# Batch 0 of a Fourier-mixing kernel: halved sums, its table transfers on another queue, some column sums moved into the main loop

## The chip, the cores and the metric

The kernel runs on one core of one Trainium2 chip. The metric is device time in microseconds (us) of one execution, the median of several. Before the change it is 1908.66 us (three runs, 1908.25 to 1909.99).

## The reference

Eight batches of 3008 x 256 numbers go through a two-dimensional Fourier transform of which the real part is kept; the result, 24064 rows of 256, goes through a gated feed-forward layer.

```python
def _attn_ref(x):                      # x: (8, 3008, 256) float32
    X = np.fft.fft(x, axis=1)
    X = np.fft.fft(X, axis=2)
    return X.real.astype(np.float32)

def _moe_ref(x, w_gate, w_val, w_out): # x: (24064, 256); weights (256, 1536), (256, 1536), (1536, 256)
    gate = 1.0 / (1.0 + np.exp(-(x @ w_gate)))
    val = x @ w_val
    return (gate * val @ w_out).astype(np.float32)
```

The weights arrive as 64-bit floating-point numbers; x and the result are float32.

## The kernel before, in words

**Stages.** Per batch the transform along the sequence is a matrix product with cosine and sine tables. The 3008 rows are folded by symmetry first, so that 753 rows (kept as 128 partitions x 6 "sets" q, row 6p + q) and 753 columns k are left; even and odd k stand apart in the tables ST[0] (cosine) and ST[1] (sine), 377 and 376 columns. The results are two arrays, pk and qk, of 128 features by 1505 frequencies. The transform along the features is never carried out: it is multiplied into w_gate and w_val ("merge"), which gives G1 and G2. The main loop then runs over 576 steps (8 batches x 6 chunks of 252 frequencies x 12 slices of the hidden width). In step i TensorE computes G1 by pk (front_a) and, a step's work later, G2 by qk on top (front_b), in a PSUM tile pf; ScalarE saves twice the first part in a tile ae (part); sums and differences of both give frequency k and its mirror image. Sigmoid (ScalarE) and products (VectorE) follow in gate_a and gate_b, and the output product comes five steps behind (back).

**E.** Feature 128 is alone in its symmetry class and has a row of its own, E, one partition high. It is written to DRAM (ed), and read back spread over 128 partitions as ek (e_rows, line 755); ScalarE starts pf with it (seed, line 765) from step 5 on. In steps 0 to 4 the first 252 of its columns (e0) are multiplied in by TensorE.

**Order.** Nothing is scheduled by a program: the order in which the source calls things is the order in each engine's queue, and each engine takes its queue strictly in order. Buffers come from pools with a fixed number of tiles per tag; a tile that is asked for again waits until all uses of the old one have ended. Matter for the change: pool hp, tag h (three buffers; the raw weight blocks 0, 1 and 2 take them first, later the gate results h), pool zp, tag z, and pool app, tag ae (two each), and the PSUM banks (three in rotation under tag x, five fixed ones po0 to po4). side, gap, mid and spare are lists of work to be issued in a given step; at(i, f) adds to the end of step i.

**The start, which the change rewrites.** Before step 0 the kernel has to

- load x of batch 0 (load_rows, line 191), the tables (load_table, line 194) and the weight blocks (weight_load, line 328), all on SP's queue in the order of the source; the table dt of the feature transform comes on ScalarE's queue;
- fold x (half_rows, line 573; VectorE) in the order of SLICES (line 485), two sets, two sets, one, one;
- turn each weight block from 64-bit to float32: weight_parts (ScalarE, lines 382 and 383), weight_join (three operations of VectorE, lines 392 to 395, then one of GpSimd, line 397);
- merge the first two blocks (merge, line 410): eight matmuls of 256 columns in the records, then two copies by ScalarE (lines 417, 418) to G2 and G1;
- sum over the sets (half, line 595): per table and per half of the columns, the even sets into one bank ev, the odd ones into another, od, 24 matmuls of 377 or 376 columns;
- add and subtract ev and od into pk and qk (places, line 611): the sum gives the near columns k, up to 752, and the difference the far ones, 1504 - k;
- the same for E (e_sums, line 696).

Every matmul is on line 133, in the helper mm, so the rows of the profile are told apart by the tiles: ev, od and pe are the sums, ps a merge, pf the front of a step, po the output. In float32 each matmul has two records.

The near columns of the first two chunks are all that the first 24 steps read.

## Time and profile before

| | |
|---|---|
| median of three runs | 1908.66 us |
| the profiled execution: its time | 1909.15 us |
| its span | 1907.4 us |
| clock granted to TensorE | 1.0 throughout |
| TensorE busy | 1895.6 us, 99% of the span |
| VectorE, ScalarE, GpSimd busy | 80%, 71%, 81% |
| first records of pf (front matmuls) | weights from 32.73, matmul from 33.05 us |
| transfers in the first 60 us | 15.58 MB |

The span runs from the first to the last recorded instruction; the 1.75 us to the execution's time lie around it. "Busy" of TensorE is modelled from the starts of pipelined matmuls. In the timeline, rows of equal instructions that follow each other are merged (x8 is eight records), and what stands in brackets is the idle time before a row and what ended it. PEld is the load of the stationary operand, which goes on beside the matmuls; SPq is SP's queue, which issues transfers. In the page's chain of waits each piece follows from what released it.

### The profile page before, as it was taken

The numbers are of one execution on the slowest core, as the hardware profiler recorded it, in microseconds if no ns is written. First come the engines' busy times: TensorE is split into PE (matmuls) and PEld (weight loads), VectorE is DVE, ScalarE is ACT, GpSimd is POOL, SyncE is SP. The second block draws the span as 40 slices with busy tenths as digits, with TensorE's granted clock in tenths as the row PEclk, the third lists the DMA queues.
The fourth block names the chain that finished last, engine by engine and source line by source line (L and its number), as shares of the span: only waits on it lengthen the run. The fifth ranks groups of instructions, "written<-read, shape, count | busy, mean of one in ns | idle before, by whom it ended". The sixth has DMA issues, their size and how long they took to land.

```text
span 1907.4 us, 36057 instructions
## 1 busy us (share of the span) xinstructions
PE 1895.6 (99%) x11836; PEld 1756.6 (92%) x11836; DVE 1520.6 (80%) x3375; ACT 1353.2 (71%) x3235; POOL 1543.4 (81%) x2733
## 2 busy tenths in 40 slices
PE   8999999999999999999999999999999999999999
PEld 5788999999999999999999999999999999999998
DVE  7678888878979778897788878888788777977775
ACT  4777777777777777777777777677767777777775
POOL 2489879987999779997799878999789986877770
PEclk9999999999999999999999999999999999999999
DMA  8446221212022121211211212122120110010001
GB/s 315 120 134 80 71 89 51 72 33 81 21 64 54 31 87 32 62 41 37 89 39 48 45 39 81 40 52 58 30 74 17 36 37 15 15 25 17 15 18 30
DMA packets 197333, 109.33 MB, mean 57 GB/s; under 512 B 134823, under 2 KB 188818, under 8 KB 195354
## 3 DMA queue, kind: packets, MB, share of 16 engines
q1 hardware_dynamic: 196568, 106.50, 21.1%
q8 instruction: 95, 1.56, 0.3%
q14 instruction: 92, 0.75, 0.1%
q10 hardware_dynamic: 546, 0.51, 0.1%
q0 software_dynamic: 32, 0.00, 0.0%
HBM read 71.24 MB, written 47.87 MB: 62 GB/s over the span
## 4 chain that ended last, share of the span: by engine, by line
PE 94%; DMA 2%; SPq 1%; POOL 1%; ACT 1%; DVE 0%; issue 0%; ACTq 0%; POOLq 0%
PE pf L133 49%; PE po L133 41%; PE sum L133 2%; DMA rtab<-in_stab_dram 1%; PE ps L133 1%; POOL sf L824 1%; DMA st<-in_stab_dram 1%; SPq L206 1%; DMA raw<-in_moe_w_val_dram 0%; PE od L133 0%; POOL x L507 0%; SPq L192 0%; SPq L375 0%; PE pe L133 0%; PE ev L133 0%
## 5 line engine op out<-in xcount | busy, mean ns | idle before, releaser
L824 POOL TENSOR_TENSOR sf<-h,sf 128x168 f32<-128x168 f32 (+1 forms) x1104 | 621.0, 582 | 79.5 <-DVE h L818 75.9
L824 POOL TENSOR_TENSOR sf<-h 128x168 f32<-128x168 f32 (+1 forms) x920 | 519.3, 584 | 159.8 <-DVE h L818 158.0
L133 PE MATMUL pf<-qk,G 128*128 128x252 f32 (+1 forms) x2304 | 583.4, 376 | 0.9 <-ACT ae L787 0.8
L133 PE MATMUL pf<-pk,G 128*128 128x252 f32 (+1 forms) x2304 | 582.7, 376 | 0.0
L772 ACT ACTIVATE pf<-ek,ge 128x252 f32<-128x252 f32 (+1 forms) x1142 | 538.2, 471 | 23.2 <-DMA ge<-G 3.0
L133 PE MATMUL po<-sf,wf 128*128 128x168 f32 (+1 forms) x2944 | 508.3, 305 | 0.0
L787 ACT ACTIVATE ae<-pf 128x504 f32<-128x504 f32 (+1 forms) x576 | 338.8, 588 | 218.7 <-PE pf L133 217.2
L133 PEld LDWEIGHTS pf<-pk,G 128*128 128x128 f32 x2304 | 435.9, 190 | 53.3 <-ACT pf L772 1.5
L133 PE MATMUL po<-h,wf 128*128 128x168 f32 (+2 forms) x2584 | 461.3, 307 | 0.0
L133 PEld LDWEIGHTS po<-sf,wf 128*128 128x128 f32 x2944 | 453.4, 190 | 8.0
L818 DVE TENSOR_TENSOR h<-pf,z 128x252 f32<-128x252 f32 (+1 forms) x576 | 240.4, 417 | 274.0 <-ACT pf L815 270.5
L802 DVE TENSOR_TENSOR z<-ae,pf 128x504 f32<-128x504 f32 (+1 forms) x576 | 384.6, 668 | 83.1 <-ACT h L801 79.1
L908 DVE TENSOR_TENSOR c<-c 128x168 f32<-128x168 f32 (+1 forms) x920 | 438.7, 500 | 3.3
L133 PEld LDWEIGHTS pf<-qk,G 128*128 128x128 f32 x2304 | 410.6, 190 | 32.3 <-ACT ae L787 2.1
L133 PEld LDWEIGHTS po<-h,wf 128*128 128x128 f32 x2584 | 410.4, 190 | 17.8 <-issue 0.9
L801 ACT ACTIVATE h<-pf 128x252 f32<-128x252 f32 (+1 forms) x576 | 216.9, 376 | 146.3 <-PE pf L133 129.0
L815 ACT ACTIVATE pf<-z 128x252 f32<-128x252 f32 (+1 forms) x576 | 214.3, 372 | 116.4 <-DVE h L814 114.5
L814 DVE TENSOR_TENSOR h<-h,pf 128x252 f32<-128x252 f32 (+1 forms) x576 | 232.9, 404 | 0.0
L824 POOL TENSOR_TENSOR sf<-sf 128x168 f32<-128x168 f32 (+1 forms) x184 | 101.7, 553 | 14.4
L824 POOL TENSOR_TENSOR sf<-sf,h 128x168 f32<-128x168 f32 (+1 forms) x184 | 110.1, 598 | 0.0
L891 ACT COPY c<-po 128x504 f32<-128x504 f32 (+1 forms) x138 | 78.5, 569 | 0.0
L918 DVE STREAM_TRANSPOSE os<-c 128x256 f32<-128x256 f32 x188 | 76.5, 427 | 0.1
(158 smaller groups left out, 876.4 us busy)
## 6 DMA issues: line engine op xcount, KB each, us to landing
x<-xr SPq DMA_DIRECT2D x14, 1536.0 KB
out_dram<-os SPq DMA_DIRECT2D x376, 56.0 KB
xr<-in_xf_dram SPq DMA_DIRECT2D x105, 128.0 KB
x<-x SPq DMA_DIRECT2D x112, 96.0 KB
xr<-in_xf_dram SPq DMA_DIRECT2D x14, 384.0 KB
ek<-ed SPq DMA_DIRECT2D x40, 126.0 KB
out_dram<-os SPq DMA_DIRECT2D x288, 7.0 KB
xr<-in_xf_dram SPq DMA_DIRECT2D x21, 124.0 KB
```

Of the source, the lines that this page charges most:

```text
L133: nc.tensor.matmul(o, l, r, start=start, stop=stop, skip_group_check=True)
L772: nc.scalar.activation(PF[i][:, g], EK[i // NFT], AF.Copy, scale=ge[:, g, f : f + 1])
L787: nc.scalar.activation(AP[i], PF[i], AF.Copy, scale=2.0)
L801: nc.scalar.activation(H[p][:, fh, 0:n], PF[i][:, 0], AF.Sigmoid)
L802: nc.vector.tensor_tensor(z[:, :, ::-1], AP.pop(i), PF[i], op=ALU.subtract)
L814: nc.vector.tensor_tensor(h[:, fh, 0:n], h[:, fh, 0:n], pf[:, 1], op=ALU.mult)
L815: nc.scalar.activation(pf[:, 0], z[:, 0], AF.Sigmoid)
L818: nc.vector.tensor_tensor(h[:, fh, n:], pf[:, 0], z[:, 1], op=ALU.mult)
L824: nc.gpsimd.tensor_tensor(block(p, dst), block(p, a), block(p, b), op=(ALU.subtract, ALU.add)[op])
L891: (nc.vector.tensor_copy if t == 1 or t == 3 else nc.scalar.copy)(C[0][:, 3 * t * R : 3 * (t + 1) * R], PO[t][:, 0 : 3 * R])
L908: nc.vector.tensor_tensor(t[:, dst * R : (dst + 1) * R], *v, op=(ALU.subtract, ALU.add)[op])
L918: nc.vector.transpose(os_[0][0][:, s, 0:nb, h, :], t[:, c0 : c0 + nb * TB])
```

## The change

All of it concerns batch 0.

- **Halved sums.** For an even row s the table's columns k and 752 - k differ by sign alone, and the sign goes with s mod 4. So only the columns from 188 up (of the even k) and up to 375 (of the odd k), H0 to H1 in the table, 377 in all, are loaded and summed for even sets, once for rows that are 0 and once for rows that are 2 modulo 4, in banks x and y; unfolded gives all columns as x + y and, mirrored, x - y. To have one kind of row in a set, sets 0 and 2 of x are loaded with the odd partitions exchanged (two transfers of 64 partitions each), and so are the table's (load_mixed). Set 4 has both kinds; its table comes as two tiles with zeros in every other partition (load_apart, in columns of wf that are free).
- **Order.** SLICES is now set 4, sets 0 and 2, set 5, set 1, set 3. The even sets of cosine and sine are summed first. E's sums stand in one place, behind the folds, on four strips of the array.
- **Queues.** x comes first on SP's queue; the even tables and one odd one are issued by ScalarE; dt and the weight blocks 0 and 1 come on SP behind x and between the last odd tables.
- **Merges** of blocks 0 and 1 stand behind the sums, one of them behind the other's join; twelve and three matmuls on a cleared tile stand before the sums (warm). The copy of e0 goes from ScalarE to VectorE.
- **Far columns** of pk, of the even k of qk, and of E, and E's way through DRAM are issued in steps 1 to 3 (E's row is read back in step 2).
- ST[0] has to be whole for the other batches' E at step 40, so its even sets are loaded again at step 35 (load_again).

```diff
-    def load_rows(q, n):
-        nc.sync.dma_start(out=X[0][0:NP, :, q : q + n], in_=xf[0, :, :, q : q + n])
-    def load_table(t, q, n, lo=0, hi=NE + NO):
-        nc.sync.dma_start(out=ST[t][0:NP, q : q + n, lo:hi], in_=stab[:, t, q : q + n, lo:hi])
+    def load_rows(*qs):
+        for q in qs:
+            for ps, r in ((slice(0, NP, 2), q), (slice(1, NP, 2), 2 - q)) if q in (0, 2) else ((slice(0, NP), q),):
+                nc.sync.dma_start(out=X[0][ps, :, q], in_=xf[0, ps, :, r])
+    H0, H1 = NE // 2, NE + NO // 2
+    def load_table(t, q, start=nc.sync.dma_start):
+        start(out=ST[t][0:NP, q], in_=stab[:, t, q])
+    def load_mixed(t):
+        for ps, qs in ((slice(0, NP, 2), slice(0, 3, 2)), (slice(1, NP, 2), slice(2, None, -2))):
+            nc.scalar.dma_start(out=ST[t][ps, 0:3:2, H0:H1], in_=stab[ps, t, qs, H0:H1])
+    apart = [[wf[:, 2 * t + h].rearrange("p m n -> p (m n)")[:, 6 * WC : 6 * WC + NE] for h in range(2)]
+             for t in range(2)]
+    def load_apart(t):
+        for h in range(2):
+            nc.scalar.dma_start(out=apart[t][h][h:NP:2], in_=stab[h::2, t, 4, H0:H1])
+    def load_again():
+        nc.sync.dma_start(out=ST[0][0:NP, 0:NQ:2], in_=stab[:, 0, 0:NQ:2])
...
-    turns = itertools.count()
+    turns = itertools.chain((2, 3), itertools.cycle((2, 3, 4)))
     def weight_use(j):
         w, c = jobs[j]
         if w == 2:
             WO[c] = WS.pop(j)
         else:
-            merge(WS.pop(j), w, c, (4, 2, 3)[next(turns) % 3] if j > 1 else None)
-    def merge(ws, g, c, other):
+            merge(WS.pop(j), w, c, HELD.pop(j) if j in HELD else bank("ps", next(turns)))
+    HELD = {}
+    def merge(ws, g, c, ps):
         cs = slice(c * WC, (c + 1) * WC)
-        ps = bank("ps", other)
...
-    SLICES = ((0, 1), (2, 3), (4,), (5,))
+    SLICES = (slice(4, 5), slice(0, 3, 2), slice(5, 6), slice(1, 2), slice(3, 4))
...
+    def unfolded(f, x, y, sn=False):
+        nc.vector.tensor_tensor(f[:, H0:H1], x[:, 0:NE], y, op=ALU.add)
+        two = [t[:, 1:NE].rearrange("p (b n) -> p b n", b=2) for t in ((y, x) if sn else (x, y))]
+        nc.vector.tensor_tensor(f[:, 0 : 2 * H1].rearrange("p (b n) -> p b n", b=2)[:, :, H0 - 1 :: -1], *two,
+                                op=ALU.subtract)
+    def seq_sums(what, x, y, od):
+        d = PQE[0][what]
+        w = [W[0, blk][what] for blk in range(2)]
+        cols = (H0, NE - H0, 0), (NE, NO // 2, NE - H0)
+        turn = {}
+        def add(n, key, o, w, tab, first=True):
+            turn[key] = turn.get(key, 0) + 1
+            mm(o, w, tab, turn[key] == 1 and first, turn[key] == n)
+        def even(*qs):
+            for q in qs:
+                for blk, (lo, n, to) in enumerate(cols):
+                    for h in range(2):
+                        if q == 4 or h == q // 2:
+                            tab = apart[what][h][0:NP, to : to + n] if q == 4 else ST[what][0:NP, q, lo : lo + n]
+                            add(2, (h, blk), (x, y)[h][:, to : to + n], w[blk][:, q], tab, blk == 0)
+        def odd(q, *blks):
+            for blk in blks or range(2):
+                lo, n = ((0, NE), (NE, NO))[blk]
+                add(3, blk + 2, od[blk][:, 0:n], w[blk][:, q], ST[what][0:NP, q, lo : lo + n])
+        def copy():
+            a = evp.tile([P, NE], F32, name="a", tag="a")
+            nc.scalar.copy(a, y[:, 0:NE])
+            return a
+        def join(a):
+            f = hp.tile([P, 6 * WC], F32, name="u", tag="h") if what else wf[:, 0].rearrange("p m n -> p (m n)")
+            unfolded(f, x, a, what)
+            return lambda blk, *ends: places(d, blk, what == 1, f[:, blk * NE : NE + blk * NO],
+                                             od[blk][:, 0 : NE - blk], ends)
+        return even, odd, copy, join
...
+    def e_first():
+        ps = bank("pe")
+        cols = (H0, NE - H0, 0), (NE, NO // 2, NE - H0)
+        turn = {}
+        def add(q, blk, band):
+            lo, n, to = cols[blk] if band < 2 else ((0, NE, 0), (NE, NO, 0))[blk]
+            tab = apart[0][band][0:NP, to : to + n] if q == 4 else ST[0][0:NP, q, lo : lo + n]
+            k = turn[band, blk] = turn.get((band, blk), 0) + 1
+            mm(ps[band * TB : band * TB + 1, to : to + n], W[0, blk][2][:, q], tab,
+               k == 1 and (blk == 0 or band > 1), k == (3 if band > 1 else 2))
+        def sums():
+            for odd, even in ((5, 0), (1, None), (3, 4)):
+                for blk in range(2):
+                    if even is not None:
+                        for h in range(2):
+                            add(even or 2 * h, blk, h)
+                    if blk == 0:
+                        for b in range(2):
+                            add(odd, b, 2 + b)
+        def unfold():
+            er = op.tile([P, NK + 1], F32, name="er", tag="os")[0:1]
+            nc.vector.memset(er[:, NK:], 0.0)
+            y, *o = (pool.tile([P, 2 * CH], F32, name=tag, tag=tag)[0:1, 0:NE]
+                     for pool, tag in ((zp, "z"), (zp, "z"), (app, "ae")))
+            for i, t in enumerate((y, *o)):
+                n = NE - i // 2
+                nc.scalar.copy(t[:, 0:n], ps[(i + 1) * TB : (i + 1) * TB + 1, 0:n])
+            f = ST[0][0:1, 4:6].rearrange("p q k -> p (q k)")
+            unfolded(f, ps[0:1], y)
+            def part(*ends):
+                for blk in range(2):
+                    places(er, blk, False, f[:, blk * NE : NE + blk * NO], o[blk][:, 0 : NE - blk], ends)
+            def end():
+                part(1)
+                nc.sync.dma_start(out=ed[0:1], in_=er)
+            part(0)
+            return er, end
+        return sums, unfold
...
-    nc.scalar.dma_start(out=dt, in_=dtab.rearrange("(c p) d -> p c d", p=P))
     load_x(0)
-    for j in range(2):
-        weight_load(j)
-    load_rows(0, 2)
-    load_table(0, 0, 2)
-    load_rows(2, 2)
-    load_table(1, 0, 2, 0, NE)
-    load_table(0, 2, 2)
-    load_rows(4, 1)
-    load_table(0, 4, 1)
-    load_rows(5, 1)
-    weight_load(2)
-    load_table(1, 2, 2, 0, NE)
-    load_table(0, 5, 1)
-    load_table(1, 4, 2, 0, NE)
-    load_table(1, 0, NQ, NE)
-    for j in (3, 5, 6, 8, 9, 4, 7):
+    idle = wf[:, 0].rearrange("p m n -> p (m n)")[:, 0 : P + WC]
+    for t in (idle, *apart[0], *apart[1]):
+        nc.vector.memset(t, 0.0)
+    load_rows(4, 0, 2, 5, 1, 3)
+    for t in range(2):
+        load_apart(t)
+    for t in range(2):
+        load_mixed(t)
+    load_table(0, 5, nc.scalar.dma_start)
+    load_table(0, 1)
+    load_table(1, 1)
+    nc.sync.dma_start(out=dt, in_=dtab.rearrange("(c p) d -> p c d", p=P))
+    weight_load(0)
+    load_table(0, 3)
+    weight_load(1)
+    load_table(1, 5)
+    load_table(1, 3)
+    for j in (2, 3, 5, 6, 8, 9, 4, 7):
         weight_load(j)
     e0 = shared["qk"][:, 4 * WC : 4 * WC + CH]
     nc.gpsimd.memset(e0, 0.0)
+    def warm(o, n):
+        for i in range(n):
+            mm(o[:, 0:WC], idle[:, 0:P], idle[:, P:], True, True)
+    warm(bank("warm", 2), 12)
+    seq_start(0)
+    folds = iter(fold_ops(0, 2))
+    od_c = [bank("od", t) for t in range(2)]
+    even, odd, copy, join = seq_sums(0, bank("u"), bank("u"), od_c)
+    e_, e_unfold = e_first()
+    od_s = [bank("od", 4)]
+    even_s, odd_s, copy_s, join_s = seq_sums(1, bank("u", 2), bank("u", 3), od_s)
+    for q, n in (((4,), 3), ((0, 2), 0)):
+        next(folds)()
+        even(*q)
+        even_s(*q)
+        warm(od_c[0], n)
+    a, a_s = copy(), copy_s()
+    next(folds)()
+    odd(5)
+    for f in folds:
+        f()
+    pk = join(a)
+    HELD[0] = bank("ps")
+    od_s.append(bank("od"))
+    odd(1)
+    odd_s(1, 1, 0)
+    odd(3)
+    for blk in range(2):
+        pk(blk, 0)
     weight_parts(0)
+    weight_join(0)
+    e_()
+    odd_s(5)
+    odd_s(3, 1)
     weight_parts(1)
-    weight_join(0)
+    weight_use(0)
+    qk = join_s(a_s)
     weight_join(1)
-    warm = bank("warm", 2)
-    for i in range(4):
-        mm(warm[:, 0:WC], dt[:, 0, 0:P], dt[:, 0], True, True)
-    weight_use(0)
+    er, e_end = e_unfold()
+    weight_parts(2)
+    nc.vector.tensor_copy(e0[0:1], er[:, 0:CH])
+    HELD[1] = bank("ps", 3)
     weight_use(1)
-    seq_start(0)
-    cos = [seq_group(0, blk, 0, (2 * blk, 2 * blk + 1)) for blk in range(2)]
-    e_, e_even = e_sums(1)
-    sin = [seq_group(0, 0, 1)]
-    for q, f in zip(SLICES, fold_ops(0, 2), strict=True):
-        f()
-        e_(*{1: (0, 1), 5: (2, 3, 4, 5)}.get(q[-1], ()))
-        sin[0][0](*{5: (3,)}.get(q[-1], ()))
-        cos[0][0](*q)
-        cos[1][0](*q)
-        sin[0][0](*{1: (0, 1), 4: (2,), 5: (4, 5)}.get(q[-1], ()))
-    places_c = [cos[blk][1]() for blk in range(2)]
-    weight_parts(2)
+    odd_s(3, 0)
     weight_join(2)
-    rest, *ends = e_even()
-    rest()
-    for f in ends:
-        f()
-    for f in places_c:
-        f()
-    nc.scalar.copy(e0[0:1], E0[0][:, 0:CH])
+    qk(0, 0)
+    qk(1, 0, 1)
     weight_parts(3)
     weight_join(3)
-    sin.append(seq_group(0, 1, 1, (0, 1)))
-    sin[1][0](*range(NQ))
     for j in range(KEEP, KEEP + 3):
         weight_load(j)
-    places_s = [group[1]() for group in sin]
-    for f in places_s:
-        f()
-    e_rows(0)
...
+    at(35, load_again)
...
+    at(1, lambda: qk(0, 1))
+    at(1, e_end)
+    at(2, lambda: e_rows(0))
+    for blk in range(2):
+        at(2 + blk, lambda blk=blk: pk(blk, 1))
```

places and the tail of e_sums (now e_joint, for the other batches alone) stay as they were; half and seq_group, which served batch 0 alone, are gone.

## The prediction

> **What bounds the kernel now.** I read the page's busy times, then its chain of waits, then the timeline and the chain of the first 60 us, because the edit touches nothing but the first four steps and one transfer at step 35.
>
> ```profile
> PE 1895.6 (99%) x11836; PEld 1756.6 (92%) x11836; DVE 1520.6 (80%) x3375; ACT 1353.2 (71%) x3235; POOL 1543.4 (81%) x2733
> ```
>
> TensorE is busy all the time, so the length is its work plus the part of the start in which it cannot work. The chain of waits over the first 60 us says where that part ends:
>
> ```profile
> 14.43 9.31 DMA st<-in_stab_dram
> ...
> 26.05 2.10 PE od L133 x6
> 28.15 0.63 PE ev L133 x2
> 28.79 0.63 PE od L133 x2
> 29.42 1.90 PE ev L133 x6
> 31.32 1.90 PE od L133 x6
> 33.21 4.25 PE pf L133 x20
> ```
>
> Up to 23.7 us transfers decide; from there TensorE runs without a pause, and the first front matmul (pf) comes at 33.0. Behind it the chain is TensorE alone (bar a stall of 0.6 us near 147 us), so a shift of the first pf reaches the end. The edit is therefore priced by when that first pf comes. Its prices stand in the timeline (start, duration):
>
> ```profile
> 5.03 0.66 ACT L382 ACTIVATE raw<-raw 128x512 f32<-128x512 f32 x1 [2.80 <-DMA raw<-in_moe_w_gate_dram]
> 5.79 3.48 PE L133 MATMUL warm<-dt 128*128 128x256 f32 x8 [5.79 <-DMA dt<-in_dtab_dram]
> ...
> 12.59 1.99 PE L133 MATMUL ps<-raw,dt 128*128 128x256 f32 x8 [1.58 <-POOL raw L397]
> ...
> 15.38 1.21 DVE L494 TENSOR_TENSOR x<-x 128x1020 f32<-128x1020 f32 x1
> ...
> 19.49 0.68 DVE L494 TENSOR_TENSOR x<-x 128x510 f32<-128x510 f32 x1
> ...
> 22.01 0.68 DVE L494 TENSOR_TENSOR x<-x 128x510 f32<-128x510 f32 x1
> ...
> 24.80 0.43 DVE L392 TENSOR_SCALAR raw<-raw 128x512 f32<-128x512 f32 x1 [0.19 <-ACT raw L382]
> 25.26 0.43 DVE L393 TENSOR_SCALAR raw<-raw 128x512 int32<-128x512 int32 x1
> 25.72 0.69 DVE L395 SCALAR_TENSOR_TENSOR raw<-raw 128x512 int32<-128x512 int32 x1
> ...
> 26.55 1.28 POOL L397 TENSOR_TENSOR raw<-raw 128x512 int32<-128x512 int32 x1 [14.02 <-DVE raw L395]
> ```
>
> From fold to fold VectorE takes 4.1 us for two sets (15.38 to 19.49) and 2.5 us for one (19.49 to 22.01). Preparing one weight block takes VectorE 0.46 + 0.46 + 0.69 us and GpSimd 1.3 us; its merge takes TensorE 1.9 us with its tail. A sum of 377 columns comes every 0.63 us. Transfers of the first 60 us, in slices of 1.5 us, keep to 361 to 416 GB/s from 4.5 to 36 us, whether their pieces are of 1, 2 or 3 KB:
>
> ```profile
> GB/s 0 105 340 408 393 416 394 382 382 398 395 376 361 367 375 381 375 384 389 388 384 395 376 392 302 204 305 351 282 14 1 3 0 6 150 119 38 60 0 0
> ```
>
> **What the change removes.** TensorE: 24 sums of 0.63 us (15.1) become 16 of half the columns and 12 whole ones. A 189-column matmul is in no row: at least half of 0.63, at most the 0.42 of the 252-column pf; I take 0.32, as the other sums go by columns. That is 5.0 + 7.6 = 12.6 us, 2.5 less. E's matmuls run four abreast on strips of the array (8 of them in 1.44 us); the 20 new ones have three of 377 columns on the longest strip, 1.9 us against 2.25 now. Transfers: 1.1 MB less ahead of the first step (12 table sets become 6 whole and 6 half ones), at 0.385 MB/us (the row below) 2.9 us less; the two weight blocks that stood first now stand behind x and most tables. Both gains count only if TensorE or the transfers still decide.
>
> **What it moves, and the new path.** Eight completion counters are dealt out in turn to the transfers of SP and ScalarE together, and an issue waits until its counter's last transfer has landed. Set 4 of x is first on SP; like the 512 KB weight block that is first now (issued 0.74, used 5.03), it lands at about 5.1. The second halves of x are issued only then: one counter is set 4's, the next an apart table's on ScalarE (issued from 2.1, behind the table load and VectorE's clears; landed 5.7). A 512 KB transfer needed 4.3 us of which 1.35 are its bytes, so 2.9 us are fixed: 256 KB issued at 5.2 land at 8.8, the next, sharing the engines with ScalarE's tables, at about 9.7. Then:
>
> - VectorE folds sets 0 and 2 together (4.1) and 5, 1, 3 one by one (7.6): 9.7 to 21.4. It is one unbroken queue, and everything below stands behind it.
> - join(a), 2 operations of 0.46 with a wait each: 22.5. The od bank of the sine is the first u bank, freed here; TensorE's sums of sets 1 and 3 mostly wait anyway.
> - two near-column sums of pk, 0.92: 23.4. The odd set 3 has to be summed by then; its table lands at 21.4 and its fold ends at 21.4, two arrivals on one point.
> - weight block 0, 1.61 + 0.15 to the hand-over: 25.2; GpSimd 1.3: 26.5. TensorE is free at the same point: set 3 (1.3) from 21.5, E (1.9), three sine sums (1.9) give 26.6.
> - merge 0, 1.9: 28.5. Now the new wait: join_s writes a tile of pool hp, whose three buffers hold the raw weight blocks 0, 1 and 2; it takes block 0's, which merge 0 reads. It begins only at 28.5, and VectorE's weight block 1 stands behind it in program order: 29.5, then 31.3; GpSimd 32.6.
> - merge 1, 1.72 to its successor: 34.4; the last sine sum 0.63: 35.1. TensorE has nothing else from 28.4 to 32.7, an idle stretch of 4.3 us that is not there now.
>
> First pf 35.2 against 33.0: **+2.2 us**. The saved 2.9 us of TensorE and the earlier tables (last one 24.8) lie in waits.
>
> **Steps 0 to 4.** E's temporaries now live until e_end at step 1: one of the two ae buffers is held, so part(1) on ScalarE has to wait until z has read AP[0] (0.68 us, VectorE, itself behind weight blocks 3, 5 and 6), and front_b(1) waits for it. Setting the listed durations in order gives a pause of about 0.8 us there: **+0.8**. Bounds: 0, if z is early, and 1.5. The five far-column operations (0.46 each, 2.3 us) and the copy of e0 that ScalarE hands to VectorE go to VectorE in steps 0 to 3, where it is idle about a third of the time (5.3 us of 10 busy from 50 to 60 us): 0 while that cover lasts, else their 2.3. E's row is written to DRAM at step 1 and read back at step 2, both on SP behind ge and the xr copies. Issued 48.5 and 53.3, it lands at 57.3, and seed(5) wants it at 57.6: hidden, with a margin near 1 us by the row's readers, and each us beyond costs one. Nothing on SP behind the read is due before.
>
> **Later.** load_again moves 1.1 MB (2.9 us) on SP at step 35; its reader, e_joint, is five steps of 3.1 us on. What stands behind it on the queue are output stores, which already wait up to 4 us without holding TensorE: 0, up to 0.5. ScalarE issues nine transfers of 0.49 us and then waits for a counter until about 8.6; its first copy is due at 15: 0. The 12 + 3 warm matmuls end before the first sums or fill a pause: 0.
>
> Sum: 2.2 + 0.8 = +3.0. The profiled execution took 1909.15 us (its span 1907.4 and 1.75 around it), 0.5 above the median 1908.66: 1912.2 in its own terms, **1911.7** as a median. From no change a measurement here tells about 0.2%, 3.8 us.
>
> **A rule against it: the clock.** The four warm matmuls took 3.48 us, the next eight-record groups 1.89: TensorE begins at half speed (though the granted clock reads 1.00 there) and is quick after about 3.3 us. A pause of 1.6 us (11.0 to 12.6) did not bring this back; no row shows one of 4.3. By these rows the sum stays +3.0. [...]
>
> **Rivals.**
>
> 1. *Transfers and TensorE still decide (faster).* If VectorE's chain lay beside them, both merges would be done when the last table lands (24.8), and four sums of 0.63 would remain: first pf at 27.4, -5.6, with +0.8 behind it 1903.9. For it: the present chain names only transfers and TensorE. Against: it decides only if weight block 1 leaves GpSimd before 24.8, 8 us sooner than the queue of folds, merge 0, join_s allows. Chance 0.04.
> 2. *The clock falls in the new pause.* Merge 1 and what follows run at half speed for 3.3 us, costing 1.7 (up to 3.4 over two stretches): 1913.4, up to 1915.1. Chance 0.25.
> 3. *64-row transfers are slow.* x sets 0 and 2 and the even tables (2.1 of 7.9 MB) go in every-other-row halves, which no row shows. At full rate nothing is added; at half rate 5.5 us, ahead of everything: 1917.2. For full rate: 32-row copies between SBUF rows with 512-byte pieces reach 190 GB/s beside other traffic, so neither end is excluded. I take full rate, since no size of piece has slowed the slices above. Chance 0.13. [...]
> 4. *Absorbed.* The start slips, but the ae pause vanishes and the stall at 147 us (0.6) takes up a part: +1.6, 1910.3. Chance 0.10.
>
> **How the numbers follow.** The forecast as worked out has 0.48; its own range is +2.0 to +4.5 (E's row late by one, the ae pause at its bounds), a third of it above 3.8. Slower by over 0.2%: 0.16 + 0.21 of rival 2 + 0.13 of rival 3 = 0.50. Faster: 0.04. Within: 0.46. The range leaves out rival 1 and the ends of 3: 1909.9 to 1916.8.
>
> **What would show it.** Right: first pf near 35; VectorE without a pause from about 10 to 25; TensorE idle some 4 us between two groups of ps, ended by GpSimd's raw; join_s right behind merge 0's end; ae of step 1 waiting for VectorE. Wrong: the ps groups close together, pf before 31 (rival 1); ps records at twice their length behind the pause (2); the first double fold beginning after 11 (3). A late e_joint or a wait for ek at step 4 would refute the zeros.

## The result, and the profile after

The kernel before took 1909.11 us (median of six runs, 1908.25 to 1910.0), the changed one 1918.18 (six runs, 1917.46 to 1919.96): 9.1 us slower, a ratio of 1.0048 with a 95% interval of 1.0035 to 1.0061. The forecast was 1911.7, its range 1909.9 to 1916.8: the sign was the likelier one, the size was three times too small and outside the range. The profiled execution took 1917.46, its span 1915.6 and 1.86 around it.

The busy times of the page say nothing of the cause; TensorE is as full as it was:

```profile
PE 1902.0 (99%) x11870; PEld 1765.9 (92%) x11870; DVE 1527.9 (80%) x3394; ACT 1351.6 (71%) x3232; POOL 1542.9 (81%) x2733
```

The chain of waits over the first 75 us (start, duration, what) shows the new path, with the pieces left out that add nothing:

```profile
1.70 4.29 DMA wf<-in_stab_dram
...
6.01 4.62 DMA x<-in_xf_dram
...
10.83 1.22 DVE x L513
...
20.11 4.30 PE od L133 x12
24.41 2.01 PE pe L133 x20
26.42 2.10 PE od L133 x6
28.51 1.74 PE ps L133 x8
30.35 0.56 DVE u L615
30.93 0.55 DVE u L617
...
32.34 0.69 DVE raw L413
...
34.50 3.78 PE ps L133 x8
38.28 1.26 PE od L133 x2
39.53 4.86 PE pf L133 x20
44.40 3.47 PE ps L133 x16
47.87 0.68 DVE z L871
48.58 0.60 ACT ae L856
49.22 1.12 PE pf L133 x4
```

To be seen: merge 0 (28.51), then join_s on VectorE (30.35), then weight block 1 (raw), then merge 1 at 34.50. Before, pf started at 33.0; now at 39.3 (the chain dates its piece from the predecessor's end). The waits of TensorE hold the pause, and the row of merge 1 its price. The waits list total, times and the longest in us; the timeline start, duration and, in brackets, the idle time before a row and what ended it:

```profile
PE ps L133 <- POOL raw L415: 4.3, 1, 4.3
```

```profile
28.35 1.89 PE L133 MATMUL ps<-raw,dt 128*128 128x256 f32 x8
30.35 0.55 DVE L615 TENSOR_TENSOR u<-u,a 128x377 f32<-128x377 f32 x1 [3.80 <-PE ps L133]
34.50 3.78 PE L133 MATMUL ps<-raw,dt 128*128 128x256 f32 x8 [4.26 <-POOL raw L415]
48.58 0.59 ACT L856 ACTIVATE ae<-pf 128x504 f32<-128x504 f32 x1 [1.49 <-DVE z L871]
49.22 1.12 PE L133 MATMUL pf<-qk,G 128*128 128x252 f32 x4 [1.37 <-ACT ae L856]
```

Eight records that took 1.89 us in merge 0 take 3.78. The windows say why (bounds, length, busy time and count of PE, PEld, DVE, ACT and POOL, then the granted clock, DMA share, GB/s):

```profile
34.00:36.00 2.00, 1.50 (x4) 1.24 (x5) 1.93 (x5) 0.00 (x0) 0.44 (x1) 0.50 0.92 317
36.00:38.00 2.00, 2.00 (x6) 1.63 (x5) 1.11 (x2) 0.00 (x0) 0.73 (x1) 0.50 0.10 23
38.00:40.00 2.00, 2.00 (x5) 1.26 (x4) 0.43 (x1) 1.68 (x4) 0.55 (x1) 0.50 0.01 0
40.00:42.00 2.00, 2.00 (x9) 1.70 (x9) 1.93 (x6) 0.20 (x2) 0.00 (x0) 0.84 0.40 42
```

From 33.8 to 40.6, 6.8 us, the clock is at half. TensorE works in 6.1 us of these, so that the pause cost its own length and then 3.1 us more. Three places serve as marks in what follows: the first pf, the second front of step 1 (the pf that waits for ae), and the first po of step 5.

| | first pf | second front, step 1 | first po, step 5 | time |
|---|---|---|---|---|
| before | 33.05 | 40.75 | 57.05 | 1909.11 |
| after | 39.33 | 49.22 | 65.58 | 1918.18 |

So in the profiled executions 6.3 us arise up to the first pf, 2.2 more up to the second front and almost none up to step 5: 8.5 in all. Then the kernel before has a pause of 0.6 us at 147 us, and the changed one has none there, so that the delay shrinks by as much:

```profile
147.84 1.12 PE L133 MATMUL pf<-qk,G 128*128 128x252 f32 x4 [0.60 <-ACT ae L787]
```

The span, which ends 3.4 us behind the last matmul instead of 3.1, is 8.2 us longer, and the time of the profiled execution 8.3. The other five runs of the changed kernel took 0.5 to 2.5 us more than the profiled one; without traces of them, the record does not show where.

### The profile page after: what moved, and what is told of

It reads as the page before. It is cut to its first block, busy times and chain, and to the rows that moved or that the text cites. A ratio compares the mean times of both kernels' runs of the same rounds, so it can differ in the third digit from the quotient of the medians.

```text
span 1915.6 us, 36162 instructions
## 1 busy us (share of the span) xinstructions
PE 1902.0 (99%) x11870; PEld 1765.9 (92%) x11870; DVE 1527.9 (80%) x3394; ACT 1351.6 (71%) x3232; POOL 1542.9 (81%) x2733
## 4 chain that ended last, share of the span: by engine, by line
PE 97%; DVE 1%; POOL 1%; DMA 0%; ACT 0%; issue 0%; ACTq 0%; DVEq 0%; POOLq 0%
PE pf L133 50%; PE po L133 42%; PE sum L133 2%; PE ps L133 1%; POOL sf L893 1%; PE od L133 0%; DMA x<-in_xf_dram 0%; DMA wf<-in_stab_dram 0%; PE pe L133 0%; POOL x L526 0%; DVE x L526 0%; DVE x L600 0%; DVE c L977 0%; DVE z L871 0%; ACT ae L856 0%
## 5 line engine op out<-in xcount | busy, mean ns | idle before, releaser
L133 PEld LDWEIGHTS po<-h,wf 128*128 128x128 f32 x2584 | 410.6, 190 | 17.5 <-issue 0.9
```

The costliest lines, as they stand in the source:

```text
L133: nc.tensor.matmul(o, l, r, start=start, stop=stop, skip_group_check=True)
```

## The experiments

My theory after the result: the chain of folds, merge 0, join_s and weight block 1 is the one foreseen; the excess is the clock, the late halves of x, and VectorE's queue up to the gate of step 1. The rivals were that the pause alone matters (not the clock), that slow half-row transfers do it, and that an earlier start is given back later. All kernels are edits of the changed one unless said, and the diffs show the parts that matter; "+" is the time above the kernel before, run beside it. The three marks are from one profiled execution each.

| kernel | first pf | second front, step 1 | first po, step 5 | + us | ratio, 95% |
|---|---|---|---|---|---|
| pause filled | 37.45 | 46.91 | 63.27 | 6.6 | 1.0024 to 1.0050 |
| pause half filled | 38.38 | 47.83 | 64.42 | 8.5 | 1.0029 to 1.0058 |
| own place for the join | 33.55 | 45.69 | 63.73 | 7.6 | 1.0027 to 1.0057 |
| block 1 ahead of the join | 35.53 | 48.01 | 64.37 | 6.9 | 1.0023 to 1.0052 |
| contiguous halves | 43.08 | 52.69 | 69.06 | 12.3 | 1.0047 to 1.0077 |
| whole sets | 39.47 | 49.36 | 65.72 | 8.0 | 1.0028 to 1.0058 |
| all loads on SP | 35.82 | 45.08 | 64.15 | 6.7 | 1.0024 to 1.0050 |
| ae buffer freed | 39.93 | 48.20 | 65.57 | 10.0 | 1.0039 to 1.0069 |
| own place and ae freed | 33.95 | 43.20 | 62.11 | 6.6 | 1.0021 to 1.0049 |
| E's copies first | 34.63 | 42.34 | 59.96 | 3.8 | 1.0011 to 1.0029 |
| and block 6, far columns later | 33.83 | 41.53 | 58.73 | 3.6 | 1.0011 to 1.0030 |
| and E's row at once | 33.92 | 41.62 | 57.93 | 1.3 | 0.9998 to 1.0017 |
| weights first | 31.58 | 42.05 | 60.14 | 4.1 | 1.0012 to 1.0031 |
| weights first, block 6 later | 31.63 | 42.09 | 59.45 | 3.7 | 1.0009 to 1.0028 |
| and E split, its row at once | 31.77 | 40.96 | 57.22 | 0.8 | 0.9995 to 1.0014 |
| and E in three places | 30.80 | 39.92 | 56.22 | -0.1 | 0.9993 to 1.0011 |
| before, with E's end late | 32.90 | 41.39 | 57.75 | 1.0 | 0.9997 to 1.0015 |

### The clock: the pause filled, and half filled

Nine idle matmuls stand in the pause; nothing on its path moves.

```diff
     weight_use(0)
+    HELD[1] = bank("ps", 3)
+    warm(HELD[1], 9)
     qk = join_s(a_s)
...
-    HELD[1] = bank("ps", 3)
     weight_use(1)
```

> The kernel after with nine matmuls on the cleared tile between merge 0 and merge 1 (some 4.2 us by 0.47 each), so that TensorE does not pause for 4.25 us. Nothing is waited for that was not before. Theory (the clock falls in the pause): granted clock 1.0 throughout, merge 1 in 1.9 us where it took 3.78, the last sine sum 0.63 where it took 1.26, first pf near 36.6 where it came at 39.33, time 2.7 us below the 1918.2 of the kernel after: 1915.5. Rival (the clock falls for another reason, such as the load of the other engines and of the transfers): the clock still reads 0.5 from 34 to 40 us, the added matmuls are long themselves, time 1918 or above.

Merge 1 came 0.5 us later than in the changed kernel, as did merge 0, and ran at full speed. From the timeline, and from the windows:

```profile
30.55 4.05 PE L133 MATMUL ps<-wf 128*128 128x256 f32 x18
34.98 1.99 PE L133 MATMUL ps<-raw,dt 128*128 128x256 f32 x8 [0.38 <-POOL raw L415]
```

```profile
34.00:36.00 2.00, 1.62 (x8) 1.11 (x7) 1.93 (x4) 0.00 (x1) 0.93 (x1) 1.00 0.93 325
36.00:38.00 2.00, 2.00 (x10) 1.57 (x9) 1.91 (x5) 0.99 (x3) 0.24 (x1) 1.00 0.11 29
```

1915.86 us, 2.3 below the changed kernel (2.5 by the column "+"): the clock's part of the 9.1, shown with the pause's path in place. With four matmuls in place of nine:

```diff
-    warm(HELD[1], 9)
+    warm(HELD[1], 4)
```

> The kernel after with four matmuls on the cleared tile behind merge 0 (1.9 us) in place of nine, so that TensorE's pause before merge 1 is some 2.4 us, not 4.25. With nine the clock stayed at 1.0 in the profiled run and the time was 1915.9. Theory (the clock falls only in pauses longer than some 3 us): clock 1.0, merge 1 in 1.9, time 1915.9. Rival (a pause between 1.6 and 4.25 us suffices in some runs; one of 2.72 us in step 1 was followed by 0.52 in one kernel and by 1.0 in another): half clock in part of the runs, times spread over 1915.9 to 1918.2.

The pause that was left was 2.52 us:

```profile
35.91 1.99 PE L133 MATMUL ps<-raw,dt 128*128 128x256 f32 x8 [2.52 <-POOL raw L415]
```

In the profiled execution the clock stayed at 1.00 behind it; it had been at half from 17.5 to 20.9, behind an earlier pause of 2.74 us for x, and merge 1 came 0.9 us later than with nine matmuls. Of the other runs, two had a mean clock of 0.998 and took 1918.0; which of the two pauses cost them the clock is not shown.

### The join's place and its order

```diff
-            f = hp.tile([P, 6 * WC], F32, name="u", tag="h") if what else wf[:, 0].rearrange("p m n -> p (m n)")
+            f = wf[:, 0].rearrange("p m n -> p (m n)")[:, what * (NE + NO) :]
```

> The kernel after with the sine's unfolded columns in free columns of wf, behind the cosine's, in place of a tile of pool hp, so that join_s has no merge to wait for. Theory (the buffer alone holds join_s, and weight block 1 behind it): join_s runs right behind the join of weight block 0, near 26.6; block 1 leaves GpSimd at 30.7 and merge 1 follows merge 0 with a pause of about 0.5 us; no fall of the clock; first pf near 33.3, 6 us earlier. The gain at the end is smaller, since ScalarE's ae and VectorE's weight blocks 2 to 6 come due earlier: 4.3 to 6 us below 1918.2, so 1912.2 to 1913.9. Rival (merge 1 is late because VectorE or the transfers are late anyway): merge 1 moves by less than 1 us and the time stays above 1917.

```diff
     weight_use(0)
-    qk = join_s(a_s)
     weight_join(1)
+    qk = join_s(a_s)
```

> The kernel after with join_s put behind the join of weight block 1: it still waits for merge 0, but nothing stands behind it that merge 1 needs. Theory (the harm is what is queued behind the waiting operation, not the wait): merge 1 close behind merge 0, near 30.3, no fall of the clock, first pf near 33, time as with a buffer of its own, 1912.2 to 1913.9. Rival (the unfolded sine columns are needed at once): the first pf comes early but the second front of step 0 waits for qk by 2 us or more, and the time stays above 1916.

With its own place the join no longer waits for merge 0 and merge 1 stood behind it with 0.67 us of idle: the buffer was the wait. The first pf came 5.8 us earlier (33.55), yet the second front only 3.5 and the time only 1.5. With the join behind block 1 it was 3.8, 1.2 and 2.2; in that profiled execution the folds also began 1.0 us later (11.83), which hides a part of the gain. Most of it was given back at the gate of step 1. From the timeline of the kernel with its own place:

```profile
45.69 1.68 PE L133 MATMUL pf<-qk,G 128*128 128x252 f32 x4 [2.72 <-ACT ae L856]
```

The pause of 1.37 had become 2.72, and a half-clock stretch followed (0.52 and 0.62 in the windows from 46 to 50; 1.00 there in the other kernel, behind a pause of the same 2.72). My reading is that VectorE, not TensorE, decides from the folds to z of step 0, and that whatever TensorE reaches earlier, it waits for there; the kernels further down test it.

### The halves of x

```diff
-            for ps, r in ((slice(0, NP, 2), q), (slice(1, NP, 2), 2 - q)) if q in (0, 2) else ((slice(0, NP), q),):
+            for ps, r in ((slice(0, HP), q), (slice(HP, NP), 2 - q)) if q in (0, 2) else ((slice(0, NP), q),):
```

> The kernel after with sets 0 and 2 of x in the same four transfers of 64 partitions, but of the lower and the upper 64 in place of every other one. The upper half of the partitions is exchanged, not the odd ones, so batch 0 is summed over the wrong rows; all work is the same. Theory A (every other partition is what makes these transfers slow): the double fold begins near 9.7 where it began at 10.83, and all behind it comes 1.1 us earlier: 1917.1. Theory B (the late issue and the sharing with ScalarE's tables make it late, not the pattern of rows): it begins at 10.6 to 10.9, time 1917.7 to 1918.6.

```diff
+            for ps, r in ((slice(0, NP), q),):
```

> The kernel after with sets 0 and 2 of x in one transfer of 128 partitions each and nothing exchanged: batch 0 is summed over the wrong rows, all other work is the same, and SP issues two transfers fewer. With the same four transfers over the lower and the upper 64 partitions these sets moved at 205 to 213 GB/s in the slices from 5 to 7 us, and the double fold began at 13.50; with every other partition it began at 10.83 and the slices read 280 to 342. Theory (64 partitions cost rate, every other one less than a contiguous half): the slices come back to 360 or more, the double fold begins near 9.7 and the time falls by 1.1 to 1917. Rival (the counters make it late): the slices stay at 280 to 342 or show a gap, the fold begins after 10.4, and the time falls by less than 0.5.

With the halves of 64 neighbouring rows the double fold began at 13.50 instead of 10.83, against what either theory said. From the timeline, and from the transfers in slices of 1.5 us:

```profile
13.50 1.22 DVE L513 TENSOR_TENSOR x<-x 128x1020 f32<-128x1020 f32 x1 [5.25 <-DMA x<-in_xf_dram]
```

```profile
GB/s 0 94 354 227 217 312 221 212 321 396 360 348 385 374 389 383 390 391 389 385 388 388 384 389 361 44 0 0 0 14 209 397 396 33 1 0 0 1 1 18
```

With neighbouring rows, four of the five slices from 4.5 to 12 us are at 212 to 227 GB/s (mean of the five 238), where the changed kernel, with every other row, has 280 to 364 (mean 322):

```profile
GB/s 0 87 360 364 280 322 303 342 337 369 378 385 371 385 389 395 390 391 382 386 388 384 388 294 30 0 0 56 363 407 223 0 1 0 0 1 7 11 1 14
```

With whole sets of x the same five slices are at 280 to 383 (mean 331), hardly more than with every other row. Why the neighbouring rows came slower is not shown.

With whole sets the double fold began at 10.68, hardly before the 10.83, and the time was 8.0 above before: every other row of x costs 1.1 us at most here. That is not rival 3's half rate; the even tables still came in every other row, and were not tried otherwise. In ten profiled kernels with exactly the changed kernel's transfers of x up to there, this fold began anywhere from 10.08 to 12.02, about 11.0 on average; the 9.7 of the forecast is outside. To see whether the order of issue sets it, all loads went on SP, with the set 5 and the odd sets of x behind the tables that are needed sooner (on top of the own place and the freed ae buffer below):

```diff
-            nc.scalar.dma_start(out=ST[t][ps, 0:3:2, H0:H1], in_=stab[ps, t, qs, H0:H1])
+            nc.sync.dma_start(out=ST[t][ps, 0:3:2, H0:H1], in_=stab[ps, t, qs, H0:H1])
...
-    load_rows(4, 0, 2, 5, 1, 3)
+    load_rows(4, 0, 2)
...
+    load_rows(5)
...
-    load_table(0, 5, nc.scalar.dma_start)
+    load_table(0, 5)
+    load_rows(1, 3)
```

> The kernel with both buffers freed, and all of x's and the tables' transfers on SP, none on ScalarE: set 4 of x, the halves of sets 0 and 2, the tables of set 4, set 5 of x, the mixed tables, then the rest. So the halves of x do not share the engines or the counters with ScalarE's tables. Theory (ScalarE's tables, which go beside them, and the counters make the halves late): all four are issued by 3 us and land near 8.5, the double fold begins there where it began at 10.83, and the folds end near 20.5; VectorE's later work and the odd tables take up a part: first pf 31.5 to 33, time 0.5 to 2 us below the kernel with both buffers freed. Rival (the transfers are the bound anyway, so that what comes sooner for x comes later for the odd tables): the double fold is early, but pk waits for the sums of set 3, and the time is that of the kernel with both buffers freed, within 0.5.

```profile
8.48 1.22 DVE L513 TENSOR_TENSOR x<-x 128x1020 f32<-128x1020 f32 x1 [1.09 <-DMA x<-in_xf_dram]
19.95 6.92 PE L133 MATMUL od<-st,x 128*128 128x377 f32 x12 [2.75 <-DVE x L602]
```

The fold came 1.6 us sooner than in the same kernel without it (10.08). The traces' times of issue and landing separate the two causes that my expectation named together. In the changed kernel the last two halves are issued at 4.98 and 6.01, each within 0.02 us of the landing of an earlier transfer on the same counter (4.96, set 4 of x; 5.99, ScalarE's first table of set 4, the 1.70 in the chain above). The records name the counters: the first eight transfers of SP and ScalarE name eight, the next eight the same ones, and of these next eight issues, at 4.98 to 8.74, six come 0.02 us behind the landing of the earlier transfer on theirs; for the other two it had landed 0.4 and 0.8 us before. With all loads on SP they are issued at 2.84 and 3.50. From issue to landing they take 5.0 and 4.6 us in the changed kernel and 4.8 and 4.9 here, without ScalarE's tables beside them. So it is the late issue behind the shared counters that this order removes. The spread of the ten is another matter: their last half is issued at 5.81 to 6.34 and takes 4.06 to 5.88 us. The time did not follow: 6.7 above before against 6.6, as the odd sets then came later (a pause of 2.75 ahead of their sums, and the clock fell there, to 0.50 from 18.9 to 25.8 us).

### The gate of step 1: ae, and then ScalarE's copies

```diff
-            y, *o = (pool.tile([P, 2 * CH], F32, name=tag, tag=tag)[0:1, 0:NE]
-                     for pool, tag in ((zp, "z"), (zp, "z"), (app, "ae")))
+            y = zp.tile([P, 2 * CH], F32, name="z", tag="z")[0:1, 0:NE]
+            o = [ST[1][0:1, 4, i * NE : i * NE + NE - i] for i in range(2)]
```

> The kernel after with E's two odd sums in unused columns of the sine table's set 4 in place of a tile of pool zp and one of pool app, so that no buffer of z or ae is held until step 1's end. Theory (the held ae buffer makes the pause of 1.4 us in step 1): ae of step 1 runs when its pf is ready, behind nothing of VectorE's; the pause goes and nothing takes its place, 1.5 us below 1918.2: 1916.7. Rival (VectorE is late with z of step 0 in any case, behind weight blocks 3, 5 and 6, and pf's three banks come free late): the pause moves to a later step, time 1917.5 to 1918.5.

The long wait for ae went, but the time did not fall. The waits of TensorE (total, times, longest):

```profile
PE pf L133 <- ACT pf L841: 0.8, 2, 0.6
PE pf L133 <- ACT ae L856: 0.8, 2, 0.6
PE pf L133 <- ACT G L437: 0.3, 1, 0.3
```

G, seed (line 841) and a later ae took its place, and the first po of step 5 came at 65.57 against 65.58: 1918.79, no faster than the changed kernel. Together with the join's own place:

> The kernel after with the sine's unfolded columns in wf and E's odd sums in the sine table's columns: neither merge 0 nor e_end holds anything. In the run with the first of the two alone the first pf came at 33.55, but ScalarE's ae of step 1 waited for VectorE for 2.72 us. Theory (what is left then is the late double fold, 1.1 us, and VectorE's work): first pf near 33.6, no pause above 0.8 us behind it, no fall of the clock, the second front of step 1 at 42 to 43 where it came at 49.22 (40.75 before): 1910.3 to 1911.3. Rival (VectorE, which joins weight blocks 2, 3, 5 and 6 in front of step 0's gate, is the bound by itself): a pause of some 2 us stays in steps 1 to 3, for a bank of pf in place of ae: 1912 to 1914.

Here VectorE and TensorE show what is late next (timeline):

```profile
32.98 0.54 DVE L615 TENSOR_TENSOR st<-pe,z 1x377 f32<-1x377 f32 x1 [2.96 <-ACT st L768]
...
44.74 0.67 DVE L871 TENSOR_TENSOR z<-ae,pf 128x504 f32<-128x504 f32 x1
...
47.95 0.69 PE L133 MATMUL pf<-pk,G 128*128 128x252 f32 x2 [1.58 <-ACT G L437]
```

VectorE idles 2.96 us for ScalarE's copies of E's sums, which stand on ScalarE behind merge 0's copies, though E's sums were long done. The next kernel is this one with those three copies issued ahead of merge 0's:

```diff
     weight_parts(1)
+    e_copies()
     weight_use(0)
```

> The kernel with both buffers freed (1915.4, first pf 33.95), and in it ScalarE's three copies of E's sums put ahead of its copies of merge 0. In that kernel VectorE stood idle for 2.96 us (to 32.98) for the last of these copies, which stood on ScalarE's queue behind merge 0, and from there to the z of step 0 at 44.74 it had no pause. Theory (VectorE's queue up to z of step 0 is the bound): VectorE's pause shrinks below 1 us, z of step 0 comes near 42.3, the pause of 1.58 us for G in step 2 goes, and the time falls by 1.5 to 2.5: 1912.9 to 1913.9. Rival (the merges or the transfers are the bound in steps 0 to 2): z comes earlier but the time stays above 1914.6.

```profile
30.63 0.53 DVE L615 TENSOR_TENSOR st<-pe,z 1x377 f32<-1x377 f32 x1
...
42.74 0.67 DVE L874 TENSOR_TENSOR z<-ae,pf 128x504 f32<-128x504 f32 x1
```

The idle time is gone and z of step 0 comes 2.0 us sooner, though the double fold began 1.9 us later in this execution (11.97 against 10.08). The kernel takes 1912.33; by the column "+" it gains 2.8 us on the last. It is the largest single step, and one that no wait of TensorE's names.

### What the late start had covered: E's row

First, weight block 6 moved behind z of step 0, and the far columns of E out of step 1 to step 7:

```diff
-                nc.sync.dma_start(out=ed[0:1], in_=er)
+                nc.sync.dma_start(out=ed[0:1, NE + NO :], in_=er[:, NE + NO :])
             part(0)
+            nc.sync.dma_start(out=ed[0:1, 0 : NE + NO], in_=er[:, 0 : NE + NO])
...
-        (pre if j in (5, 6) else join).setdefault(0 if j == 6 else i, []).append(lambda j=j: weight_join(j))
+        (pre if j == 5 else join).setdefault(i, []).append(lambda j=j: weight_join(j))
...
-    at(1, e_end)
+    at(7, e_end)
```

> The kernel with both buffers freed and E's copies first, and in it E's two far-column operations in step 7 in place of step 1 (E's near columns go to DRAM as soon as they are there), and VectorE's join of weight block 6 behind z of step 0 in place of before it. Theory (what VectorE does before it reaches each step's gate sets steps 1 to 3, so the far columns are not free there): z of step 0 another 2.5 us earlier, z of step 1 not behind 1.6 us of E's row, time 1 to 2 us below the kernel with E's copies first: 1911 to 1912.5. Rival (only z of step 0 counts, or merge 6 is late in its place): within 0.5 of that kernel.

The second front came 0.8 sooner, and 0.2 of it was left in the time. The rows of step 4 tell why: the read-back ek was issued at 52.7, the seed that takes it and ge ran at 56.74 behind an idle time of 1.54 that the trace puts down to ge, and TensorE waited for the seed:

```profile
56.74 0.98 ACT L845 ACTIVATE pf<-ek,ge 128x252 f32<-128x252 f32 x2 [1.54 <-DMA ge<-G]
57.77 1.12 PE L133 MATMUL pf<-pk,G 128*128 128x252 f32 x4 [0.62 <-ACT pf L845]
```

In the changed kernel the seed ran at 63.0 without a wait for ek. Reading the row back directly behind its writing:

```diff
             nc.sync.dma_start(out=ed[0:1, 0 : NE + NO], in_=er[:, 0 : NE + NO])
+            e_rows(0)
...
-    at(2, lambda: e_rows(0))
```

> The kernel with block 6 later (1912.15), and in it E's row is read back from DRAM as soon as its near columns are written there, in place of in step 2. In that kernel TensorE waited 0.62 us in step 5 for ScalarE's seed, which copies that row. Theory (with the start shortened, the read-back in step 2 comes too late, so that its zero was only cover): the wait goes, 0.6 to 0.9 us less: 1911.2 to 1911.6. Rival (the seed is late for ScalarE's own queue): the wait stays and the time is within 0.3 of 1912.15.

The same matmul ran at 57.08 with no wait. ge was issued at 53.26 against 53.41, hardly sooner, and the seed ran at 55.19 instead of 56.74: it had waited for ek. The time is 1910.43, lower by 1.7 between the medians and 2.3 by the column "+" (the kernel before was itself 0.6 slower beside this one); between the two profiled executions it is 1.0, and 0.8 at the first po of step 5. The margin that I had taken to be 1 us was the late start's own. The same part alone, in the kernel before:

```diff
-    for f in ends:
-        f()
+    ends[0]()
...
-    e_rows(0)
...
+    at(1, ends[1])
+    at(2, lambda: e_rows(0))
```

> The kernel before with one part of the change alone: E's last far-column operation and E's way to DRAM in step 1, its read-back in step 2. As in the change, a buffer of z and one of ae are held until step 1's end. By the prediction's steps: a pause of 0.8 us for ae in step 1 (0 to 1.5) and nothing for the read-back, 1909.4 (1908.6 to 1910.1). Other theory (both cost more where VectorE is busy up to the gate): a pause of 1.5 to 2.5 for ae and one of 0.5 or more for the seed in step 5, 1910.6 to 1911.6.

```profile
41.39 1.12 PE L133 MATMUL pf<-qk,G 128*128 128x252 f32 x4 [0.63 <-ACT ae L787]
```

From the first pf to the second front it took 8.49 us against 7.70, so 0.8 for the held ae buffer, as forecast; the time was 1.0 above before, with an interval that just reaches zero.

### Weights first, as in the kernel before

Blocks 0 and 1 and dt load ahead of x again, and are prepared and merged in VectorE's wait for x; the cosine's join stands ahead of the last fold.

```diff
     load_x(0)
+    nc.scalar.dma_start(out=dt, in_=dtab.rearrange("(c p) d -> p c d", p=P))
+    for j in range(2):
+        weight_load(j)
...
-    warm(bank("warm", 2), 12)
+    warm(bank("warm", 2), 6)
+    for j in range(2):
+        weight_parts(j)
+        weight_join(j)
+    for j in range(2):
+        weight_use(j)
```

> Halved sums with the order of before for the weights: dt and weight blocks 0 and 1 are loaded first, joined while VectorE waits for x, and merged before the sums; x and the tables follow on SP, all buffers freed, E's copies first, E's far columns in step 7, the cosine's unfolding ahead of the last fold. Theory (moving the two blocks behind the folds is what costs, since VectorE's 3.2 us for them lay in a wait before): x's folds begin some 2.5 to 3 us later than in the kernel after and end near 25, but nothing but pk, qk and E stands between them and the first pf, which comes at 30 to 32; VectorE reaches z of step 0 near 40 to 41 as before; time 1908 to 1910. Rival (x later by two blocks' transfers gives the gain back): folds end after 26.5, time 1912 or above.

> As the kernel with the weights first, and VectorE's join of weight block 6 behind z of step 0 in place of before it. Theory (VectorE's queue in front of z is the bound): z of step 0 another 2 us earlier, 38 to 39, and the time 0.5 to 1.5 us below the kernel with the weights first, 1907 to 1909, which would be level with the kernel before or below it. Rival (TensorE or the transfers are the bound there): the same time as with the weights first, within 0.4.

The second of the two has block 6 moved as above. The first pf came at 31.6, before the 33.05 of the kernel before; then TensorE stood again. From the timeline of the second:

```profile
31.63 1.01 PE L133 MATMUL pf<-pk,G 128*128 128x252 f32 x4
34.34 1.12 PE L133 MATMUL pf<-wqk,G 128*128 128x252 f32 x4 [1.70 <-DVE wqk L1093]
```

The first front's second part needs e0, E's row in wqk, and VectorE writes it late. Both are level with the kernel that leaves the weights behind (4.1 and 3.7 against 3.8 and 3.6), so the weights' order is worth nothing by itself. With E's sums mostly ahead of the last fold and its row read back at once:

```diff
-    odd_s(5)
+    e_((5, 0), (1, None))
     next(folds)()
     odd(3)
-    e_()
+    e_((3, 4))
...
+    odd_s(5)
     odd_s(3, 1)
```

> The kernel with the weights first and block 6 later (1912.2; first pf 31.63, then TensorE waited 1.70 for E's columns and 0.83 in step 5 for the seed), and in it E's sums of all sets but the last stand ahead of the last fold, the sine's sums of set 5 behind E's, and E's row is read back at once. Theory (E's sums in one place behind the folds are what the first front then waits for): the second pair of pf comes 1.5 us earlier, near 32.9, the seed's wait goes, and the time falls by 2 to 2.5: 1909.7 to 1910.2, still 1.2 to 1.7 above before. Rival (VectorE's joins decide): pf comes earlier, a pause of 1 to 2 us opens at the merges behind it, 1911 to 1912.

1910.01; the wait for e0 was 0.43. Last, E's sums in three places, each behind a fold, the cosine's join ahead of the last two folds, and block 2 prepared ahead of E's columns:

```diff
-    next(folds)()
     pk = join(a)
     od_s.append(bank("od"))
+    e_((5, 0))
+    odd_s(5, 1, 0)
+    next(folds)()
     odd(1)
-    odd_s(1, 1, 0)
-    e_((5, 0), (1, None))
+    e_((1, None))
+    odd_s(1, 1)
```

> The kernel with the weights first and E split (1910.0; first pf 31.77, TensorE waited 0.43 us for E's columns and 0.53 for GpSimd's weight block 3), and in it E's sums in three places, each right behind a fold, the cosine's unfolding ahead of the last two folds, the sine's sums of set 5 ahead of the fold of set 1 (its table is loaded two places earlier), and VectorE's join of weight block 2 ahead of E's columns. Theory (what TensorE and VectorE still do behind the last fold is what stands between this kernel and a gain): the second pair of pf comes 1 us earlier, near 32.2, no wait for weight block 3, the time 1 to 1.5 us lower, 1908.5 to 1909.0, level with before or 0.5 below it. Rival (the transfers, whose last tables land near 25 us, and the time outside the span decide): within 0.4 of 1910.0.

1908.23 against 1908.36: nine microseconds below the changed kernel by the column "+" and level with the one before (1.0002, 0.9993 to 1.0011). It reaches the first pf 2.2 us sooner than before and pays 1.15 at e0 and 0.3 at ae:

```profile
30.80 1.01 PE L133 MATMUL pf<-pk,G 128*128 128x252 f32 x4
32.96 1.12 PE L133 MATMUL pf<-wqk,G 128*128 128x252 f32 x4 [1.15 <-DVE wqk L1098]
39.92 1.06 PE L133 MATMUL pf<-qk,G 128*128 128x252 f32 x4
56.22 1.85 PE L133 MATMUL po<-h,wf 128*128 128x504 f32 x4
```

The first po of step 5 is 0.8 sooner than before. Over the runs, side by side, the median span is 0.3 us shorter (1906.3 against 1906.6), but the median time around it is 2.0 us against 1.8, and no gain is left; two of the eleven runs took 1911.1, with a mean clock of 0.998. In the kernel before with E's end late, 1.8 lie around the span; in the changed kernel and all its edits the medians are 1.9 to 2.2: the excess comes with the changed start. What it is was not found.

## Why the prediction was wrong

- **The path was right.** join_s waits for merge 0, block 1 stands behind it, GpSimd's raw ends TensorE's pause (4.26 us against the forecast 4.3), ae of step 1 waits for VectorE. The own place for the join shows that the buffer is the wait. Rival 1 did not happen: the first pf did not come early. Of rival 4 one half did: the 0.6 us pause at 147 us is gone in the changed kernel and took up that much of the delay; the ae pause did not vanish.
- **The step that failed first: the clock in the new pause taken as no change** (rival 2, 0.25). From merge 1 to its successor it took 3.57 us against 1.72, the last sine sum 1.26 against 0.63, and the first group of pf 1.50 against 0.85: 3.1 us together. The filled pause puts the clock at 2.3 to 2.5 us of the kernel's time, within the 1.7 to 3.4 that the rival gave. "A pause of 1.6 us did not bring this back" was the only row, and I let it speak for 4.3.
- **The x halves at 9.7 were mis-sized:** the double fold began at 10.83, in its siblings at 10.08 to 12.02. The folds ended at 22.57 instead of 21.4, merge 0 at 30.25 instead of 28.5. Of the 1.75 us at merge 0's end 1.1 are the fold's start; the rest is the sums between, which ended at 28.35 instead of 26.6. The path of the halves was the foreseen one, with the issue behind two landings (6.01, forecast 5.7). The term that was too small is the transfer: 4.6 us from issue to landing, where the step from 5.7 to 9.7 left it 4.0, and 0.2 from there to the fold. Rival 3 looked at the pattern of the rows; whole sets show that of x to be worth 1.1 at most.
- **The pause for ae at 0.8 was right for what it described** (0.79 in the kernel before) and too small here (1.37), since in the changed kernel VectorE's queue up to z was later still. One part of that may be two operations of weight preparation that took 1.20 and 1.40 us there beside GpSimd, where the kernel before has one of 1.41 (last section): 0.8 us more on that queue, which no run tested. I followed VectorE to the first pf and then summed durations; the runs show that the same queue decides up to the second front, so that even removing the 4.3 us pause bought 1.5.
- **Two zeros held only under cover.** The read-back of E's row cost nothing while the start was late; it is worth 0.8 in the marks and 1.7 to 2.3 in the time once the start is not. ScalarE's copies of E, not in the sum at all, stood behind merge 0's and were worth 2.8 once the join was free. load_again showed no cost: from step 5 to the end the delay does not grow. Nor did ScalarE's time for its issues: its first copy, at 16.66, waited for TensorE. E's far columns, moved to step 7 together with block 6, gave 0.2 us; the other far columns were not moved.
- **The range.** The clock, the late merge 0 and the longer ae wait hold together; I had priced the first two as rivals that exclude each other, with no case for their sum. With the measured sizes it is 3.0 + 3.1 + 1.75 + 0.6 = 8.45, against the 8.5 at step 5.

What stays open: why the transfer of a half takes 4.06 us in one execution and 5.88 in another, where the runs of the changed kernel differ by 2.5 us, and the 0.2 us around the span.

## What to carry to other kernels

When a change leaves an engine's queue as the path, follow that queue to the first point where the loop's next step waits for it, not to the first instruction of the loop: here, of 3.5 to 5.8 us gained ahead of the first pf, 1.5 to 2.5 were left in the time, and the rest came back as waits for ae and G. A pause of about 2 us or more on TensorE is priced with the half-clock stretch that may follow it (here 3.41 or 6.83 us behind most pauses of 2.1 us and more). Rivals that can happen together belong into one sum before the range is drawn, and a step costed at nothing has to be asked again once its cover moves.

## What I had not expected of the hardware

- **Half-clock stretches came in one length or its double, on a fixed grid.** In these traces each of the 18 ahead of the last matmul lasted 3.41 or 6.83 us (6.83 in the changed kernel, from 33.81 to 40.64). Pauses of 2.98 to 4.92 us were always followed by one, pauses of 2.1 to 2.8 mostly (not behind 2.52 in one profiled execution and 2.72 in another), those of 1.6 to 1.9 never. The traces show what sets them apart. Behind the first 5 us of an execution all falls and returns of the clock lie whole steps of 3.41 us apart (with the join's own place it fell at 15.38 and at 46.09, nine steps). Cut along these steps, the slot that ends in a fall has TensorE standing for 1.86 us or more in all 18 falls (for the whole 3.41 in the changed kernel, from 30.40 to 33.81), and no slot with 1.85 or less ends in one. The pauses of 2.52 and 2.72 fell across a step, with at most 1.36 and 1.85 us on one side. The stretch lasted 3.41 us when TensorE stood for no more than 0.2 us of the slot after the fall (10 times), and 6.83 when it stood for 0.64 or more (8 times; 0.68 in the changed kernel). So, as an estimate from these 18, a pause of twice 1.86 us, or 3.72, would cost the clock in this start wherever it falls, and the 4.26 was no matter of chance.
- **64 neighbouring rows of x came slower than every other row**, a mean of 238 GB/s in the slices from 4.5 to 12 us against 322; whole sets of x reach 331 there.
- **VectorE was slower beside GpSimd.** Single operations of weight preparation (lines 410 and 411, before 392 and 393) took 1.20 to 1.41 us instead of 0.42 where GpSimd's last step of a weight block (line 415, before 397) ran beside them, and 0.55 to 0.87 beside its end, in both kernels (1.20 at 43.07 and 1.40 at 45.83 us in the changed one, 1.22 at 7.84 and 1.41 at 38.12 in the one before). That GpSimd is the cause was not tested.
